# Contiguous host layouts for x, v and the first weights; the inverse's products in row-major order in DRAM; a spilled filter read in pieces of eight k1

## The chip, the cores and the metric

The kernel runs on one core of one Trainium2 chip. The metric is the time of one execution in microseconds of device time; several executions are taken and their median is given. A separate execution is recorded by the hardware profiler, and its span, from the first to the last instruction, is what all rows of the trace below refer to.

## What is computed

A long convolution, gated, and two token-wise MLPs behind it (T = 12480 tokens, D = 128 channels, d_ff = 2048):

```python
h_mlp = np.maximum(pos_emb @ w1, 0.0) @ w2
h_filt = h_mlp * np.exp(-0.01 * pos)[:, None]
u = x * v
y = irfft(rfft(u, 2 * S) * rfft(h_filt, 2 * S))[:S]
x = (x * y)
x = relu(x @ w_in) ** 2 @ w_out                 # moe
h = x @ w_in2
out = (h * sigmoid(1.702 * h)) @ w_out2          # moe2
```

The weights of the MLPs arrive as 64-bit floats; x, v and the filter's inputs as 32-bit floats.

## The kernel before

The convolution is done as a Fourier transform of length N1 x N2 = 99 x 127 in two steps, with real matrices on TensorE; the symmetric and antisymmetric halves (64 values j each) are kept apart. The stages follow each other on TensorE:

1. **Filter stage** (`filter_stage`, lines 192 to 257). Sixteen steps of four j: `stage2` multiplies the position features with w1, VectorE writes `htsb`; `stage3` multiplies with `w2s` and `w2d` (w2 twice, and w2 with its second half negated, made by VectorE at lines 224 and 225) and fills `h`. Beside it the class `Inputs` (lines 152 to 190) brings in x and v in 16 chunks of eight channels: `load` issues four DMAs a chunk (rows 0 to 95 and 96 to 98 of x and of v), `multiply` forms x*v and the even part of u on GpSimd, `odd` the odd part on VectorE. There are four buffers for x and v, and a new chunk is only asked for when the chunk four before it has had its `odd`.
2. **First transform of h** (lines 541 to 552, `s1_step`, 32 steps of four channels). Each four steps fill one `Ah`, which is written to DRAM (`ahd`, line 551). `Ah` has two buffers, so step 8 has to wait for the write of steps 0 to 3. The write is issued by SP, in order with the loads of x and v: the first stands behind the load of chunk 12, the second behind that of chunk 14.
3. **First transform of u** (lines 557 to 562, 32 steps), into `A` in SBUF. Meanwhile SP fetches the first matrices `m` and the first pieces `Hs` of the spilled filter.
4. **Second transform, product and inverse** (`stage_s2`, lines 286 to 351): 50 pairs p of frequencies k1. `spectra` multiplies `Hs` and `A` with `m` on TensorE and copies one result on ScalarE; `product` forms the complex product (VectorE, and one part on GpSimd) one pair later; `back` multiplies by the inverse matrix two pairs later, and ScalarE copies the result to `bs`, which goes to DRAM (`bd`) every two pairs (line 334). `load_m` asks for the matrices of pair p+4, `load_h` (line 279) at each odd p for the Hs of four k1 (two pairs) with number p//2+2, into one of three buffers. VectorE also converts the first MLP's weights from 64 bits here, step by step (`Weights.tick`, one step a pair); their raw chunks are fetched by `load_raw` (line 83).
5. **The MLPs** (`mlp`, lines 385 to 524). For each of 26 tiles of 480 tokens, `load_b` (line 372) reads the products `bd` back as `uv`, in 32 pieces, GpSimd forms `b`, `front_y` finishes the inverse on TensorE, and then eight units of matrix products a layer run, three passes each.

All orders are written out by hand; an engine and a DMA queue take their instructions in program order. SP issues the loads (but for w2 and two small ones) and the writes of `Ah`; ScalarE's queue issues the writes of `bd` and of the output. Lines are those of the kernel before.

Of the kernel before, what the change touches and what calls it, by code (L numbers as in the profile page):

```python
# [9 lines left out]
FP32 = mybir.dt.float32  # L10
F32R = mybir.dt.float32r
I32 = mybir.dt.int32
U32 = mybir.dt.uint32
ACTF = mybir.ActivationFunctionType
ALU = mybir.AluOpType
# [12 lines left out]
D = 128  # L28
F = 64
DFF = 2048  # L30
NP = -(-N1 // 2)
DC = 16
NDC = D // DC
XC = 8
NXC = D // XC
HK = 4
NHK = -(-N1 // HK)
JG = 2
MW = 480
NTILE = T // MW  # L40
# [20 lines left out]
def conv_mlp_kernel(ctx: ExitStack, tc: tile.TileContext, xc, xt, vc, pt, w1, w2,  # L61
# [10 lines left out]
    wj = const.tile([128, NJ], FP32, name="wj")  # L72
    sign = const.tile([128, 2], FP32, name="sign")

    bd = dram.tile([N1, 2, NJ, 2, D], FP32, name="bd")
    ahd = dram.tile([128, NDC, N1, 2, DC], FP32, name="ahd")
    raws = [moe_w_in, moe_w_out.rearrange("(k p) e -> p k e", p=128),
            moe2_w_in, moe2_w_out.rearrange("(k p) e -> p k e", p=128)]
    WC = 512
    NWC = DFF // WC  # L80
    wts = []

    def load_raw(n, pool):
        i, c = divmod(n, NWC)
        raw = pool.tile([128, WC, 2], I32, tag="raw", name="raw", bufs=2)
        if i % 2 == 0:
            nc.sync.dma_start(out=raw.rearrange("p a b -> p (a b)"),
                              in_=raws[i].bitcast(I32)[:, c * 2 * WC:(c + 1) * 2 * WC])
        else:
            k = WC // 128  # L90
            nc.sync.dma_start(out=raw.rearrange("p (k e) b -> p k (e b)", k=k),
                              in_=raws[i].bitcast(I32)[:, c * k:(c + 1) * k, :])
        return raw
# [58 lines left out]
    class Inputs:  # L152
# [6 lines left out]
        def load(self):  # L159
            c = self.loaded  # L160
            if c == NXC or c - self.odd_done == 4:
                return
            self.loaded += 1
            sl = slice(c * XC, (c + 1) * XC)
            xs, vs = (self.pool.tile([N1, XC, 2, NJ], FP32, tag=n, name=n, bufs=4) for n in ("x", "v"))
            for r in (slice(0, ROWS), slice(ROWS, N1)):
                nc.sync.dma_start(out=xs[r], in_=xc[r, sl])
                nc.sync.dma_start(out=vs[r], in_=vc[r, sl])
            self.tiles[c] = xs, vs

        def multiply(self):
# [20 lines left out]
    def filter_stage(fp, bank, h, inputs):  # L192

        HC = 4
        NC_ = NJ // HC
        bw1 = fp.tile([128, 128], FP32, name="bw1", bufs=1)
        w2s = fp.tile([128, D], FP32, name="w2s", bufs=1)
        w2d = fp.tile([128, D], FP32, name="w2d", bufs=1)
        warm = fp.tile([128, 1], FP32, name="warm", bufs=1)
        nc.vector.memset(bw1, 0.0)  # L200
        nc.vector.memset(warm, 0.0)
        p_t, ht_t = {}, {}

        def load_pos(c):
            p = fp.tile([128, HC, N1], FP32, tag="pos", name="pos", bufs=12)
            nc.sync.dma_start(out=p, in_=pt[:, c * HC:(c + 1) * HC, :])
            p_t[c] = p

        nc.scalar.activation(out=warm, in_=warm, func=ACTF.Sigmoid)
        for i in range(2):  # L210
            nc.sync.dma_start(out=bw1[i * F:(i + 1) * F, i * F:(i + 1) * F], in_=w1)
        for c in range(4):
            load_pos(c)
        for i in range(2):
            nc.scalar.dma_start(out=w2s[i * F:(i + 1) * F], in_=w2)
        nc.scalar.dma_start(out=wj, in_=c_w2)
        nc.scalar.dma_start(out=wn1, in_=c_w1)
        for c in range(4, 8):
            load_pos(c)
        inputs.load()  # L220
        nc.sync.dma_start(out=cs1, in_=c_s1)
        nc.vector.memset(sign[:, 0:1], 1.0)
        nc.vector.memset(sign[:, 1:2], -1.0)
        nc.vector.tensor_copy(out=w2d[0:F], in_=w2s[0:F])
        nc.vector.tensor_scalar(out=w2d[F:128], in0=w2s[F:128], scalar1=-1.0, scalar2=None, op0=ALU.mult)

        def stage2(c):
            ps = bank("hp")[:, 0:HC * N1].rearrange("p (j n) -> p j n", n=N1)
            nc.tensor.matmul(out=ps, lhsT=bw1, rhs=p_t.pop(c))
            sb = fp.tile([128, HC, N1], FP32, tag="ht", name="htsb")  # L230
            wb = wj[:, c * HC:(c + 1) * HC].unsqueeze(2).to_broadcast([128, HC, N1])
            nc.vector.scalar_tensor_tensor(out=sb, in0=ps, scalar=0.0, in1=wb, op0=ALU.max, op1=ALU.mult)
            ht_t[c] = sb

        def stage3(c):
            sb = ht_t.pop(c)
            ps = bank("op")[:N1].rearrange("p (s d j) -> p s d j", s=2, j=HC)
            for j in range(HC):
                for s, w in enumerate((w2s, w2d)):
                    nc.tensor.matmul(out=ps[:, s, :, j], lhsT=sb[:, j, :], rhs=w)  # L240
            nc.vector.tensor_scalar(out=h[:, :, c * HC:(c + 1) * HC], in0=ps[:, 0], scalar1=wn1[:, 0:1],
                                    scalar2=None, op0=ALU.mult)
            nc.scalar.activation(out=h[:, :, NJ + c * HC:NJ + (c + 1) * HC], in_=ps[:, 1],
                                 func=ACTF.Copy, scale=wn1[:, 0:1])

        for c in range(NC_ + 1):
            if c + 8 < NC_:
                load_pos(c + 8)
            if c < NC_:
                stage2(c)  # L250
                inputs.load()
            if c >= 1:
                stage3(c - 1)
            if c >= 1:
                inputs.multiply()
            if c in (6, 8, 9, 11, 12, 14, 16):
                inputs.odd()
# [19 lines left out]
        nc.sync.dma_start(out=m_t[p][:, 0:n], in_=c_s2[:, 2 * p:2 * p + n])  # L277

    def load_h(mp, g):
        if g >= NHK:  # L280
            return
        n = min(HK, N1 - g * HK)
        h_t[g] = mp.tile([128, NDC, HK, 2, DC], FP32, tag="Hs", name="Hs", bufs=3)
        nc.sync.dma_start(out=h_t[g][:, :, 0:n], in_=ahd[:, :, g * HK:g * HK + n])

    def stage_s2(sp, mp, A, hooks, work):

# [8 lines left out]
        with kp as kp, obp as obp:  # L296
            def spectra(p):
                n, m = pair(p), m_t[p]
                xk, hk = (kp.tile([128, 2, 2, D], FP32, tag=t, name=t) for t in ("xk", "hk"))
                for j in range(n):  # L300
                    k = 2 * p + j
                    nc.tensor.matmul(out=hk[:, j].rearrange("p c (q d) -> p q c d", d=DC),  # L302
                                     lhsT=m[:, j, 0, :], rhs=h_t[k // HK][:, :, k % HK])
                    nc.tensor.matmul(out=xk[:, j], lhsT=m[:, j, 0, :], rhs=A[:, k])  # L304
                hc = sp.tile([128, 2, 2, D], FP32, tag="hc", name="hc", bufs=2)
                nc.scalar.copy(out=hc[:, 0:n], in_=hk[:, 0:n])
                k_t[p] = xk, hc
# [16 lines left out]
            def back(p):  # L324
                n, m, P = pair(p), m_t.pop(p), P_t.pop(p)
                ob = obp.tile([128, 2, 2, D], FP32, tag="ob", name="ob")
                for j in range(n):
                    nc.tensor.matmul(out=ob[:, j], lhsT=m[:, j, 1, :], rhs=P[:, j])  # L328
                g, o = divmod(2 * p, HK)
                if o == 0:  # L330
                    bs_t[g] = sp.tile([128, HK, 2, D], FP32, tag="bs", name="bs", bufs=2)
                nc.scalar.copy(out=bs_t[g][:, o:o + n], in_=ob[:, 0:n])
                if o + n == HK or p == NP - 1:
                    nc.scalar.dma_start(
                        out=bd[HK * g:HK * g + o + n].rearrange("k h j c d -> (h j) k c d"),
                        in_=bs_t.pop(g)[:, 0:o + n])

            for p in range(NP + 2):
                if p < NP:
                    spectra(p)  # L340
                if 0 <= p - 2:
                    back(p - 2)
                load_m(mp, p + 4)
                if p % 2 == 1:
                    load_h(mp, p // 2 + 2)
                if 0 <= p - 1 < NP:
                    product(p - 1)
                work.tick(p)
                for f in hooks.get(p, ()):
                    f()  # L350
# [21 lines left out]
    def load_b(bp, t):  # L372


        last = max(p[0] for p in tile_parts(t)) // JG
        for k in range(loaded[0], last + 1):
            uv = bp.tile([N1, 2, JG, 2, D], FP32, tag="uv", name="uv", bufs=2)
            nc.sync.dma_start(out=uv, in_=bd[:, :, k * JG:(k + 1) * JG])
            b = bp.tile([N1, JG, 2, 2, D], FP32, tag="b", name="b", bufs=3)
            for s, c, op in ((0, 0, ALU.subtract), (0, 1, ALU.add), (1, 0, ALU.add), (1, 1, ALU.subtract)):  # L380
                nc.gpsimd.tensor_tensor(out=b[:, :, s, c], in0=uv[:, 0, :, c], in1=uv[:, 1, :, 1 - c], op=op)  # L381
            b_t[k] = b
        loaded[0] = last + 1
# [268 lines left out]
```

## Time and profile before

| | us |
|---|---|
| runs: median (lowest to highest) of 3 | 1493.61 (1490.3 to 1494.48) |
| profiled execution: its own time | 1490.39 |
| profiled execution: span | 1488.2 |
| TensorE busy | 1436.5 |
| VectorE busy | 1151.8 |
| ScalarE busy | 953.4 |
| GpSimd busy | 272.4 |

The busy time of an engine is the time in which it had an instruction running; idle time costs something only where the engine that sets the pace of a stage is the idle one. The execution's own time is 2.2 us longer than the span. TensorE is busy for 97% of the span, and its idle time lies in the first 325 us.

### The profile page before, as it was taken

Reading aid. Unit: us, or ns where it says so; the run is one execution under the profiler, and the core shown is the slowest. Engines: PE = TensorE matmul, PEld = TensorE weight load, DVE = VectorE, ACT = ScalarE, POOL = GpSimd, SP = SyncE. Lnnn points to the kernel's source line nnn. Section 1 sums busy time; section 2 is a strip of 40 time slices with the busy share of each in tenths; the row PEclk is TensorE's granted clock in tenths of the full one; section 3 lists DMA queues with packets and bytes.
Section 4 is the critical chain, followed back from the end, with each engine's and each line's share of the span. In section 5 each row is a group of like instructions: output and inputs, shape, how many; then the busy total and the mean of one; then the engine's idle time right before and its main releaser. Section 6 shows DMA issues by size and latency. Waiting matters only on the chain.

```text
span 1488.2 us, 17857 instructions
## 1 busy us (share of the span) xinstructions
PE 1436.5 (97%) x6994; PEld 1243.6 (84%) x6994; DVE 1151.8 (77%) x1306; ACT 953.4 (64%) x1108; POOL 272.4 (18%) x230
## 2 busy tenths in 40 slices
PE   8899988869999999999999999999999999999998
PEld 7799777758878888888888888888888888888887
DVE  5677898949988777777777777777777777777887
ACT  2355443437756677666677667677666677667776
POOL 4930322232461111111101111201112001000000
PEclk9999999979999999999999999999999999999999
DMA  9872899731210000000000000000100000000000
GB/s 227 260 314 65 255 289 292 244 106 58 78 50 29 25 7 25 25 29 25 25 7 25 25 29 25 25 8 24 36 18 25 25 8 24 7 1 7 14 14 14
DMA packets 73934, 103.71 MB, mean 70 GB/s; under 512 B 5524, under 2 KB 56026, under 8 KB 72826
## 3 DMA queue, kind: packets, MB, share of 16 engines
q1 hardware_dynamic: 56620, 83.11, 18.4%
q10 hardware_dynamic: 17230, 19.47, 3.6%
q8 instruction: 55, 0.90, 0.2%
q14 instruction: 29, 0.24, 0.1%
HBM read 70.22 MB, written 32.34 MB: 69 GB/s over the span
## 4 chain that ended last, share of the span: by engine, by line
PE 83%; DMA 9%; DVE 4%; POOL 2%; issue 1%; ACT 1%; SPq 0%; POOLq 0%; ACTq 0%; DVEq 0%
PE acc L428 12%; PE hin L429 12%; PE acc L430 12%; PE hin L430 12%; PE hin L428 12%; PE acc L429 11%; DMA Hs<-ahd 5%; PE s L264 4%; PE yps L416 4%; DMA x<-in_xc_dram 2%; PE hk L302 2%; PE xk L304 2%; PE ob L328 1%; DVE gl L465 1%; POOL b L381 1%
## 5 line engine op out<-in xcount | busy, mean ns | idle before, releaser
L465 DVE TENSOR_TENSOR gl<-g,gh 128x960 fp32r<-128x960 f32 x416 | 490.9, 1180 | 35.9 <-ACT gh L461 35.4
L445 ACT ACTIVATE g<-hin 128x960 f32<-128x960 f32 x208 | 202.5, 973 | 239.1 <-PE hin L430 238.3
L428 PE MATMUL acc<-gh,w 128*128 128x480 f32 x832 | 319.6, 384 | 0.6 <-DVE lo L404 0.6
L428 PE MATMUL hin<-hi,w 128*128 128x480 f32 x832 | 318.0, 382 | 1.4 <-ACT hi L403 1.4
L429 PE MATMUL hin<-lo,w 128*128 128x480 f32 x832 | 317.4, 381 | 0.4 <-DVE lo L404 0.4
L430 PE MATMUL acc<-gh,w 128*128 128x480 f32 x832 | 317.6, 382 | 0.0
L430 PE MATMUL hin<-hi,w 128*128 128x480 f32 x832 | 317.0, 381 | 0.0
L429 PE MATMUL acc<-gl,w 128*128 128x480 f32 x832 | 316.1, 380 | 1.0 <-DVE gl L465 1.0
L381 POOL TENSOR_TENSOR b<-uv 99x256 f32<-99x256 f32 x128 | 164.3, 1314 | 774.9 <-DMA uv<-bd 483.2
L456 DVE TENSOR_TENSOR g<-hin,g 128x960 f32<-128x960 f32 x208 | 239.8, 1153 | 57.7 <-ACT g L448 57.6
L454 DVE CAST gh<-g 128x960 fp32r<-128x960 f32 x208 | 142.6, 686 | 154.4 <-ACT g L446 154.3
L448 ACT ACTIVATE g<-hin 128x960 f32<-128x960 f32 x208 | 201.0, 966 | 84.0 <-PE hin L430 75.7
L446 ACT ACTIVATE g<-g 128x960 f32<-128x960 f32 x208 | 209.4, 1007 | 6.6
L461 ACT CAST gh<-g 128x960 fp32r<-128x960 f32 x208 | 204.5, 983 | 0.3 <-DVE g L456 0.3
L428 PEld LDWEIGHTS hin<-hi,w 128*128 128x128 f32 x832 | 156.6, 188 | 29.5 <-ACT g L445 3.3
L429 PEld LDWEIGHTS acc<-gl,w 128*128 128x128 f32 x832 | 156.5, 188 | 29.0 <-DVE gl L465 3.1
L429 PEld LDWEIGHTS hin<-lo,w 128*128 128x128 f32 x832 | 157.0, 189 | 25.9 <-DVE lo L404 0.9
L430 PEld LDWEIGHTS acc<-gh,w 128*128 128x128 f32 x832 | 156.4, 188 | 26.3
L428 PEld LDWEIGHTS acc<-gh,w 128*128 128x128 f32 x832 | 156.3, 188 | 26.2 <-DVE lo L404 1.0
L430 PEld LDWEIGHTS hin<-hi,w 128*128 128x128 f32 x832 | 156.6, 188 | 25.7
L416 PEld LDWEIGHTS yps<-ci,b 99*128 99x128 f32 x608 | 75.3, 198 | 15.3 <-POOL b L381 13.7
L416 PE MATMUL yps<-ci,b 99*128 99x98 f32 (+19 forms) x608 | 75.4, 279 | 12.0 <-POOL b L381 12.0
(58 smaller groups left out, 1185.8 us busy)
## 6 DMA issues: line engine op xcount, KB each, us to landing
ahd<-Ah SPq DMA_DIRECT2D x8, 1584.0 KB
uv<-bd SPq DMA_DIRECT2D x32, 396.0 KB
m<-in_c_s_dram SPq DMA_DIRECT2D x49, 256.0 KB
Hs<-ahd SPq DMA_DIRECT2D x24, 512.0 KB
bd<-bs ACTq DMA_DIRECT2D x24, 512.0 KB
xs<-in_xt_dram SPq DMA_DIRECT2D x26, 240.0 KB
out_dram<-o ACTq DMA_DIRECT2D x26, 240.0 KB
x<-in_xc_dram SPq DMA_DIRECT2D x16, 384.0 KB
```

The lines of the kernel that those rows point to most:

```text
L381: nc.gpsimd.tensor_tensor(out=b[:, :, s, c], in0=uv[:, 0, :, c], in1=uv[:, 1, :, 1 - c], op=op)
L416: nc.tensor.matmul(out=ps[:, o:o + w], lhsT=b[:, c, :], rhs=ci2[:, c, r:r + w], start=(c == 0), stop=(c == 1))
L428: nc.tensor.matmul(out=out, lhsT=a, rhs=hl[0], start=first, stop=False)
L429: nc.tensor.matmul(out=out, lhsT=a, rhs=hl[1], start=False, stop=False)
L430: nc.tensor.matmul(out=out, lhsT=b, rhs=hl[0], start=False, stop=last)
L445: nc.scalar.activation(out=g, in_=ps, func=ACTF.Relu)
L446: nc.scalar.activation(out=g, in_=g, func=ACTF.Square)
L448: nc.scalar.activation(out=g, in_=ps, func=ACTF.Sigmoid, scale=1.702)
L454: nc.vector.tensor_copy(out=gh, in_=g)
L456: nc.vector.tensor_tensor(out=g, in0=ps, in1=g, op=ALU.mult)
L461: nc.scalar.copy(out=gh, in_=g)
L465: nc.vector.tensor_tensor(out=gl, in0=g, in1=gh.bitcast(FP32), op=ALU.subtract)
```

## The change

Six edits. (1) The host lays x and v out as [chunk, row, channel, half, j], so that one chunk of eight channels is one contiguous stretch; each row's piece keeps its 4 KB, but the rows, which lay 64 KB apart, now lie 4 KB apart. (2) The two `w_in` are laid out in four chunks of 512 columns, each contiguous; a row's piece keeps its 4 KB and the pitch goes from 16 KB to 4 KB. (3) `bd` is laid out as [half, j, k1, part, channel] in place of [k1, half, j, part, channel]: a write of four k1 has one piece of 4 KB a partition in place of four of 1 KB, and a read has pieces of 1 KB in place of 2 KB, next to each other in place of 128 KB apart. (4) A load of `uv` becomes two DMAs, one for each half. (5) `Hs` holds eight k1 (four pairs) in place of four, in two buffers in place of three, and is asked for at p = 3, 7, 11, ...; the piece goes from 512 B to 1 KB. (6) VectorE makes `w2d` after its first step of `stage2` instead of before it.

```diff
-    bd = dram.tile([N1, 2, NJ, 2, D], FP32, name="bd")
+    bd = dram.tile([2, NJ, N1, 2, D], FP32, name="bd")
...
             nc.sync.dma_start(out=raw.rearrange("p a b -> p (a b)"),
-                              in_=raws[i].bitcast(I32)[:, c * 2 * WC:(c + 1) * 2 * WC])
+                              in_=raws[i].bitcast(I32)[c])
...
-            sl = slice(c * XC, (c + 1) * XC)
             xs, vs = (self.pool.tile([N1, XC, 2, NJ], FP32, tag=n, name=n, bufs=4) for n in ("x", "v"))
             for r in (slice(0, ROWS), slice(ROWS, N1)):
-                nc.sync.dma_start(out=xs[r], in_=xc[r, sl])
-                nc.sync.dma_start(out=vs[r], in_=vc[r, sl])
+                nc.sync.dma_start(out=xs[r], in_=xc[c, r])
+                nc.sync.dma_start(out=vs[r], in_=vc[c, r])
...
-        nc.vector.tensor_copy(out=w2d[0:F], in_=w2s[0:F])
-        nc.vector.tensor_scalar(out=w2d[F:128], in0=w2s[F:128], scalar1=-1.0, scalar2=None, op0=ALU.mult)
...
                 stage2(c)
                 inputs.load()
+            if c == 0:
+                nc.vector.tensor_copy(out=w2d[0:F], in_=w2s[0:F])
+                nc.vector.tensor_scalar(out=w2d[F:128], in0=w2s[F:128], scalar1=-1.0, scalar2=None,
+                                        op0=ALU.mult)
...
-        if g >= NHK:
+        if g >= NHL:
             return
-        n = min(HK, N1 - g * HK)
-        h_t[g] = mp.tile([128, NDC, HK, 2, DC], FP32, tag="Hs", name="Hs", bufs=3)
-        nc.sync.dma_start(out=h_t[g][:, :, 0:n], in_=ahd[:, :, g * HK:g * HK + n])
+        n = min(HL, N1 - g * HL)
+        h_t[g] = mp.tile([128, NDC, HL, 2, DC], FP32, tag="Hs", name="Hs", bufs=2)
+        nc.sync.dma_start(out=h_t[g][:, :, 0:n], in_=ahd[:, :, g * HL:g * HL + n])
...
-                                     lhsT=m[:, j, 0, :], rhs=h_t[k // HK][:, :, k % HK])
+                                     lhsT=m[:, j, 0, :], rhs=h_t[k // HL][:, :, k % HL])
...
-                        out=bd[HK * g:HK * g + o + n].rearrange("k h j c d -> (h j) k c d"),
+                        out=bd[:, :, HK * g:HK * g + o + n].rearrange("h j k c d -> (h j) k c d"),
...
-                if p % 2 == 1:
-                    load_h(mp, p // 2 + 2)
+                if p % 4 == 3:
+                    load_h(mp, p // 4 + 2)
...
-            nc.sync.dma_start(out=uv, in_=bd[:, :, k * JG:(k + 1) * JG])
+            for h in range(2):
+                nc.sync.dma_start(out=uv[:, h], in_=bd[h, k * JG:(k + 1) * JG].rearrange("j k c d -> k j c d"))
...
-    laid['xc'] = _folded(x).transpose(0, 3, 1, 2)
-    laid['vc'] = _folded(v).transpose(0, 3, 1, 2)
+    for name, a in (('xc', x), ('vc', v)):
+        laid[name] = _folded(a).transpose(3, 0, 1, 2).reshape(NXC, XC, N1, 2, NJ).transpose(0, 2, 1, 3, 4)
+    for name in ('moe_w_in', 'moe2_w_in'):
+        laid[name] = inputs[name].reshape(D, NWC, WC).transpose(1, 0, 2)
```

Here HL = 8, NHL = 13, HK = 4, DC = 16, JG = 2.

How the order of the issues moves is shown at three places. The first is SP's queue in the second transform; `m` is the matrices of a pair, `Hs` a piece of the spilled filter, `raw` a chunk of raw weights. Before:

```order
L87 DMA raw<-in_moe_w_in_dram 128x1024
L277 DMA m<-in_c_s_dram 128x512
L284 DMA Hs<-ahd 128x8x128
L277 DMA m<-in_c_s_dram 128x512 x2
L284 DMA Hs<-ahd 128x8x128
L277 DMA m<-in_c_s_dram 128x512 x2
L284 DMA Hs<-ahd 128x8x128
L91 DMA raw<-in_moe_w_out_dram 128x4x256
L277 DMA m<-in_c_s_dram 128x512 x2
L284 DMA Hs<-ahd 128x8x128
```

The same place with the change:

```order
L88 DMA raw<-in_moe_w_in_dram 128x1024
L279 DMA m<-in_c_s_dram 128x512 x3
L286 DMA Hs<-ahd 128x8x256
L279 DMA m<-in_c_s_dram 128x512 x2
L92 DMA raw<-in_moe_w_out_dram 128x4x256
L279 DMA m<-in_c_s_dram 128x512 x2
L286 DMA Hs<-ahd 128x8x256
L279 DMA m<-in_c_s_dram 128x512 x4
L286 DMA Hs<-ahd 128x8x256
```

An Hs stood behind every second m and now stands behind every fourth, with twice the bytes. The second place is SP's queue where the MLPs begin; `xs` is a tile of x for the gating. Before:

```order
L378 DMA uv<-bd 99x2x512 x2
L87 DMA raw<-in_moe_w_in_dram 128x1024
L370 DMA xs<-in_xt_dram 128x480
L378 DMA uv<-bd 99x2x512
L91 DMA raw<-in_moe_w_out_dram 128x4x256
```

The same place with the change:

```order
L381 DMA uv<-bd 99x2x256 x4
L88 DMA raw<-in_moe_w_in_dram 128x1024
L372 DMA xs<-in_xt_dram 128x480
L381 DMA uv<-bd 99x2x256 x2
L92 DMA raw<-in_moe_w_out_dram 128x4x256
```

Four issues stand ahead of the raw chunk in place of two, with the same bytes in all. The third place is the start of VectorE's work. Before:

```order
L223 MEMSET sign 128x1
L224 COPY w2d<-w2s 64x128
L225 TENSOR_SCALAR w2d<-w2s 64x128
L232 SCALAR_TENSOR_TENSOR htsb<-hp,wj 128x396 x2
L241 TENSOR_SCALAR h<-op,wn_62 99x128x4
```

The same place with the change:

```order
L223 MEMSET sign 128x1
L230 SCALAR_TENSOR_TENSOR htsb<-hp,wj 128x396
L251 COPY w2d<-w2s 64x128
L252 TENSOR_SCALAR w2d<-w2s 64x128
L230 SCALAR_TENSOR_TENSOR htsb<-hp,wj 128x396
L239 TENSOR_SCALAR h<-op,wn_62 99x128x4
```

The two instructions on w2d have moved behind the first htsb.

## Rows read from the trace of the kernel before

**Rows 1.** The page's part 4, the chain that ended last, by line

```profile
PE acc L428 12%; PE hin L429 12%; PE acc L430 12%; PE hin L430 12%; PE hin L428 12%; PE acc L429 11%; DMA Hs<-ahd 5%; PE s L264 4%; PE yps L416 4%; DMA x<-in_xc_dram 2%; PE hk L302 2%; PE xk L304 2%; PE ob L328 1%; DVE gl L465 1%; POOL b L381 1%
```

**Rows 2.** Windows: stretch, length, busy PE, PEld, DVE, ACT, POOL, clock, DMA share, GB/s

```profile
0.00:40.00 40.00, 34.84 (x238) 29.27 (x238) 20.51 (x36) 9.73 (x14) 18.73 (x19) 1.00 0.92 228
40.00:80.00 40.00, 31.35 (x180) 29.18 (x178) 21.96 (x28) 13.83 (x19) 39.30 (x29) 0.91 0.90 279
...
148.00:300.00 152.00, 132.69 (x592) 110.72 (x592) 137.37 (x214) 62.28 (x108) 43.32 (x50) 1.00 0.85 268
300.00:325.00 25.00, 15.14 (x62) 12.64 (x63) 6.00 (x7) 7.23 (x9) 11.95 (x16) 0.60 0.47 143
...
454.00:1488.00 1034.00, 1030.27 (x4940) 888.83 (x4938) 797.38 (x809) 731.46 (x812) 103.67 (x88) 1.00 0.06 20
```

**Rows 3.** Timelines of ACT and PE, 48 to 84 us: start, length, instructions, idle before

```profile
67.99 2.96 ACT L266 COPY Ah<-s 64x792 f32<-64x792 f32 x4 [7.00 <-DMA ahd<-Ah]
78.37 2.96 ACT L266 COPY Ah<-s 64x792 f32<-64x792 f32 x4 [7.42 <-DMA ahd<-Ah]
...
48.70 9.65 PE L264 MATMUL s<-cs,h 99*128 99x198 f32 x56 [1.56 <-ACT h L243]
...
69.88 7.86 PE L264 MATMUL s<-cs,h 99*128 99x198 f32 x32 [4.08 <-DVE Ah L268]
80.26 4.04 PE L264 MATMUL s<-cs,h 99*128 99x198 f32 x14 [2.52 <-DVE Ah L268]
```

**Rows 4.** SP in order of time, 58 to 70 us

```profile
58.62 0.32 SPq L167 DMA_DIRECT2D x<-in_xc_dram  x1
...
60.16 0.36 SPq L551 DMA_DIRECT2D ahd<-Ah  x1
...
69.68 0.35 SPq L551 DMA_DIRECT2D ahd<-Ah  x1
```

**Rows 5.** GpSimd in order of time, 37 to 59 us

```profile
37.01 2.51 POOL L178 TENSOR_TENSOR x<-x,v 99x512 f32<-99x512 f32 x2 [2.95 <-DMA v<-in_vc_dram]
...
56.82 1.77 POOL L180 TENSOR_TENSOR u<-x 99x512 f32<-99x512 f32 x1
```

**Rows 6.** DMA queues, 10 to 50 us: packets, MB, share of 16

```profile
q1 hardware_dynamic: 3556, 9.59, 96.9%
```

**Rows 7.** DMA queues of 341 to 345 us, one weight chunk alone

```profile
q1 hardware_dynamic: 144, 0.52, 44.5%
```

**Rows 8.** DMA queues of 88 to 106 us, mostly writes of Ah

```profile
q1 hardware_dynamic: 464, 5.07, 67.5%
```

**Rows 9.** Waits of 148 to 300 us: in total, times, longest

```profile
PE hk L302 <- DMA Hs<-ahd: 16.2, 16, 2.2
DVE t L315 <- ACT hc L306: 12.5, 16, 2.4
```

**Rows 10.** VectorE in order of time, 150 to 158 us

```profile
150.24 1.29 DVE L315 TENSOR_TENSOR t<-xk,hc 128x512 f32<-128x512 f32 x2 [1.84 <-ACT hc L306]
...
156.38 1.29 DVE L315 TENSOR_TENSOR t<-xk,hc 128x512 f32<-128x512 f32 x2 [0.84 <-ACT hc L306]
```

**Rows 11.** The chain that ended last in order of time: two of eleven loads of Hs

```profile
157.33 5.97 DMA Hs<-ahd
...
248.16 7.45 DMA Hs<-ahd
```

**Rows 12.** DMA queues of 160 to 290 us (q10 is ScalarE's queue)

```profile
q1 hardware_dynamic: 31579, 26.19, 67.3%
q10 hardware_dynamic: 11281, 11.19, 24.4%
```

**Rows 13.** The chain in order of time at the change of stage

```profile
299.20 2.54 DMA bd<-bs
301.87 5.29 DMA uv<-bd
```

**Rows 14.** Instructions on tile uv: least, median, longest ns

```profile
L378 SPq DMA_DIRECT2D uv<-bd x32: 780/801/936, 301.9 to 1227.2; - x32
```

More of the change, by code (lines that the diff above doesn't have):

```diff
@@ L30 @@
 DFF = 2048
+WC = 512
+NWC = DFF // WC
 NP = -(-N1 // 2)
@@ L36 @@
 HK = 4
-NHK = -(-N1 // HK)
+HL = 8
+NHL = -(-N1 // HL)
 JG = 2
@@ L78, in conv_mlp_kernel @@
             moe2_w_in, moe2_w_out.rearrange("(k p) e -> p k e", p=128)]
-    WC = 512
-    NWC = DFF // WC
     wts = []
```

## The prediction

> **What bounds the kernel now.** I read the chain that ended last first, to see which transfers are on it: loads of Hs hold 5% of the span and loads of x 2% [rows 1], though part of that time TensorE works beside them. Next come the stretches of the stages: from 454 us on TensorE is busy for 1030.27 of 1034 us, so nothing that a DMA does can shorten the MLPs [rows 2]. Time can only be won ahead of 325 us, in three places.
>
> Place A, 60 to 82 us, is the first transform of h. ScalarE may not fill the third and fourth `Ah` until the writes of the first and second have landed: 7.00 and 7.42 us [rows 3]. TensorE rests for 4.08 and 2.52 us of this, and is slow behind it: 56 matmuls in 9.65 us are 0.172 us each when it is not held up, so the 32 in 7.86 us lose 2.35 us and the 14 in 4.04 us lose 1.63 us [rows 3]; the granted clock of the stretch 40 to 80 us is 0.91 [rows 2]. Together TensorE loses 4.08 + 2.52 + 2.35 + 1.63 = 10.6 us. The write is late because SP issues it behind the load of chunk 12 (58.62, then 60.16 us), and the second behind chunk 14 (69.68 us) [rows 4]. That load waits for a buffer which GpSimd frees: chunk 8 ends at 56.82 + 1.77 = 58.59 us [rows 5]. GpSimd works without a pause from 37.01 us, and started there because v of chunk 4 had not come (2.95 us of waiting) [rows 5]. So the rate of the x and v loads before 37 us sets the time of the writes.
>
> Place B, 148 to 300 us, is the second transform. TensorE waits for Hs 16 times, 16.2 us, but VectorE, 137.37 us busy of 152, is the fuller engine, and it waits for the copy of that product 12.5 us in 16 waits [rows 2, 9]. The first two of these, 1.84 and 0.84 us, are the start of the pipeline [rows 10]; 9.8 us are left that come from Hs. A load takes 5.97 to 7.45 us from issue to landing [rows 11]. It is asked for at p = 2g-3 and needed at p = 2g, so two whole pairs lie between, 2 x 2.65 = 5.3 us (132.69 us over 50 pairs) [rows 2]: too few.
>
> Place C, 299 to 308 us, is the change to the MLPs: the last write of bd takes 2.54 us and the first uv 5.29 us, one after the other [rows 13].
>
> **The change part by part.** The sum is made on the profiled execution, 1490.39 us. The three runs shown have a median of 1493.61; the four times together average 1492.2, and I start from that: the profile gives the differences, 1492.2 the level.
>
> Hs in eights: SP issues 13 loads in place of 25. The load at p = 4g-5 is needed at p = 4g, four whole pairs later, which is 4 x 2.75 = 11.0 us at VectorE's pace (137.37 / 50). A load has 0.52 MB more, 2.0 us at 268 GB/s [rows 2], so it lands after 8.0 to 9.5 us (5.97 and 7.45 plus 2.0). It is in time by 1.5 us or more, and the 9.8 us vanish; VectorE is then the bound and no more than that can come. The DMA engines must keep up: in 160 to 290 us the two queues took 67.3% + 24.4% = 91.7% of 16 engines for 37.4 MB [rows 12]. In 121 us the same packet time would be 98.5%. Half the packets of Hs and a quarter of those of bd make it less; at the rate of long pieces (below, 26 KB/us an engine) it would be 74%. I take 9 us, nearly all, as the lead is certain and the room small; the ends are 0 and 9.8, and a loss is a rival below.
>
> x and v contiguous: from 10 to 50 us the engines were full, 0.969 x 16 x 40 = 620 engine-us for 9.59 MB, which is 15.5 KB/us an engine [rows 6]. A weight chunk, alone, with the same 4 KB pieces but 16 KB apart, took 0.445 x 16 x 4 = 28.5 engine-us for 0.52 MB, 18.2 KB/us [rows 7]. Writes with pieces of 12.7 KB ran at 5.07 MB in 194 engine-us, 26.1 KB/us [rows 8]. Those three are the bounds: no gain, 18.2, and 26.1. I take 18.2, the row nearest in piece and direction. The first five chunks are 5 x 0.81 = 4.06 MB: 262 engine-us become 223, and 39 / 16 = 2.4 us; at 26.1 it would be 6.6 us. GpSimd's unbroken row begins 2.4 us earlier, and with it SP's issue of the writes. Chunks 12 to 15 share the engines with the first two writes; their 3.24 MB cost 209 engine-us and would cost 178, 1.9 us less ahead of the second write. I take 2.4 + 1.9, rounded down to 4 us. The ends are 0 and 10.6, all that is lost in place A. Nothing is late next: GpSimd and then TensorE go on without a gap.
>
> One rule speaks against this term. The Trainium skill, "DMA: Bandwidth & Descriptors", section on latency and other measured facts, says that a row pitch of large powers of two slows HBM, with full rate still at 512 KiB and a loss from 2 MiB on. By it 64 KB costs nothing, and the 4 us would be 0. The rows show a slower stream at 64 KB than at 16 KB [rows 6, 7], though not that the pitch is the reason.
>
> bd and uv: a write of bd takes a quarter of the packets; it lies beside other work except for the last one. The last uv is on the path. Its issue costs 0.80 us [rows 14], and a second issue adds up to 0.8 us ahead of GpSimd; two for the second piece, 1.6 us. Against that stand pieces next to each other: if it landed as fast as bd's write, 2.54 in place of 5.29 us [rows 13], 2.75 us would be saved. I take 0, between -1.9 and +1.6. Later uv loads are hidden by the MLPs' 1030 us of matmuls [rows 2]; 32 more issues on SP, 26 us over 1034, have nobody behind them in a hurry.
>
> w_in in contiguous chunks: VectorE is not seen waiting for a raw chunk, so 0; what hides it is the conversion of the chunk before. w2d behind the first htsb: VectorE is busy 20.51 of 40 us there [rows 2], and the first consumer comes behind w2s; 0.
>
> The sum is 9 + 4 + 0 = 13 us: 1477.4 on the profiled execution, 1479 at the level of 1492.2.
>
> **The rivals.**
> 1. The layout of x and v brings nothing, since the distance of the rows is not what makes the stream slow. Then 1492.2 - 9 = 1483. The rule of the Trainium skill named above would have it so. For it: the mixed stream of 10 to 50 us has other loads in it. Against: the row of the weight chunk.
> 2. Place B brings nothing, as the DMA engines are full and the same bytes take the same time; Hs stays late in another rhythm. Then 1492.2 - 4 = 1488. For it: 98.5% above. Against: fewer packets.
> 3. Neither does what it says: 1492.
> 4. Slower. An Hs of 1.05 MB, with a raw chunk of 0.52 MB ahead of it, holds up what stands behind it on SP's queue, the m of the next pairs. If SP's queue got only half of the 268 GB/s while ScalarE's queue writes bd, the two take 11.7 us and 2.5 us to land, 14.2 in all, 3.2 us over the 11.0 of lead. Seven raw chunks make 22 us, five loads without one 1 us each: 27 in place of 9.8, so 1492.2 + 17 - 4 = 1505. It decides from about 185 GB/s on SP's queue downward (1.57 MB in 8.5 us). Against: over 130 us that queue had 26.19 MB, 201 GB/s [rows 12], and the bytes of a raw chunk come once in six pairs.
>
> **How the numbers follow.** My forecast has a chance of 0.62, rival 1 0.18, rival 2 0.08, rival 3 0.07, rival 4 0.05. A measurement of this kernel can tell about 0.3%, 4.5 us, from no change: the border lies near 1488. Forecast and rival 1 are faster, half of rival 2 too: 0.84. The other half and rival 3 are within: 0.11. Slower is rival 4: 0.05. With both terms at their upper ends the time is 1492.2 - 20.4 = 1472, with uv's end 1470 and the level 2 us lower 1468. The upper end takes in rivals 1 and 2: 1488. Left out are rivals 3 and 4 and some of the tails, under 2 in 10.
>
> **What would show it.** Right: in 148 to 300 us TensorE waits for Hs 3 us or less in sum, and VectorE for `hc` about 3 us; the stage ends about 9 us sooner after its start. GpSimd's unbroken row starts near 34.5 us, the first write of Ah is issued near 57.5 us, ScalarE's two waits shrink to about 4 to 6 us each. From 10 to 50 us the engines move 18 KB/us or more. Wrong: waits for m in the second transform (rival 4), waits for Hs of the old size (rival 2), 15.5 KB/us again (rival 1), or a first uv that lands later than 7 us after its issue.

## The result, and the profile after

| | before | after |
|---|---|---|
| runs: median (lowest to highest), us | 1491.95 (1490.21 to 1494.48), 4 runs | 1477.49 (1476.27 to 1478.08), 4 runs |
| profiled execution: its own time, us | 1490.39 | 1478.08 |
| profiled execution: span, us | 1488.2 | 1475.9 |

The ratio is 0.9902, with a 95% interval of 0.9886 to 0.9918: 14.5 us by the medians, 12.3 us by the two profiled spans. The forecast was 1479.0. In the chain that ended last, loads of Hs held 5% of the span and of x 2% [rows 1]; neither is among its lines now. For Hs that is the gain shown below. For x it is not: the chain of the kernel after still holds loads of x and v for 23% of its first 110 us, a little under 1% of the span each. The page's part 4 of the kernel after, by line:

```profile
PE acc L431 12%; PE acc L433 12%; PE hin L432 12%; PE hin L433 12%; PE hin L431 12%; PE acc L432 12%; PE yps L419 4%; PE s L266 4%; PE ob L330 2%; DVE t L317 1%; PE xk L306 1%; PE hk L304 1%; DMA ahd<-Ah 1%; POOL b L384 1%; DVE gl L468 1%
```

Shares do not say where the 12.3 us are. I cut both executions at the same four events: the first product `hk` of the second transform, the issue of the last write of `bd`, and the first `yps` of the MLPs.

| stretch | before, us | after, us | less by |
|---|---|---|---|
| span's start to first `hk` (place A in it) | 147.11 | 146.74 | 0.4 |
| first `hk` to last issue of `bd` (place B) | 299.20 - 147.11 = 152.1 | 287.81 - 146.74 = 141.1 | 11.0 |
| last issue of `bd` to first `yps` (place C) | 308.10 - 299.20 = 8.9 | 294.96 - 287.81 = 7.15 | 1.75 |
| first `yps` to the end | 1180.1 | 1180.9 | -0.8 |

**Place B.** The waits of the second transform, in the stretch 130 to 300 us of the kernel after (engine, line and what it waited for; us in total, times, longest):

```profile
POOL P L321 <- DVE t L317: 75.8, 41, 2.5
...
PE ob L330 <- POOL P L321: 5.2, 11, 1.4
...
DVE t L317 <- ACT hc L308: 2.7, 2, 1.8
...
PE hk L304 <- DMA m<-in_c_s_dram: 0.9, 1, 0.9
```

There is no wait for Hs any more; before it was 16.2 us on TensorE [rows 9]. VectorE waited 16 times for `hc`, 12.5 us; two waits of 2.7 us are left, the two that belong to the start of the pipeline [rows 10]. TensorE now waits for the products `P`, which GpSimd makes behind VectorE's `t`. One window over exactly this stretch (columns as in [rows 2]):

```profile
146.70:287.80 141.10, 133.87 (x594) 111.81 (x594) 136.22 (x214) 61.96 (x108) 43.32 (x50) 0.99 0.82 281
```

VectorE is busy for 136.22 of 141.10 us: it is the bound, as foreseen. The stage's 11.0 us are the 9.8 us of waits and 1.2 us by which VectorE's own work became shorter (137.42 us over the same stretch before). The DMA queues, 160 to 280 us (packets, MB, share of 16 engines):

```profile
q1 hardware_dynamic: 20152, 25.65, 66.2%
q10 hardware_dynamic: 3179, 11.56, 23.6%
```

25.65 MB in 0.662 x 16 x 120 engine-us is 20.2 KB/us an engine; before it was 18.7 (26.19 MB in 0.673 x 16 x 130, [rows 12]). ScalarE's queue went from 22.0 to 25.5.

**Place A.** ScalarE and TensorE in order of time, 66 to 89 us of the kernel after, to be held against [rows 3] (start, length, instructions, and in brackets the idle time before):

```profile
67.06 2.96 ACT L268 COPY Ah<-s 64x792 f32<-64x792 f32 x4 [6.37 <-DMA ahd<-Ah]
77.40 2.96 ACT L268 COPY Ah<-s 64x792 f32<-64x792 f32 x4 [7.38 <-DMA ahd<-Ah]
...
68.95 8.96 PE L266 MATMUL s<-cs,h 99*128 99x198 f32 x32 [3.45 <-DVE Ah L270]
79.29 2.95 PE L266 MATMUL s<-cs,h 99*128 99x198 f32 x16 [1.38 <-DVE Ah L270]
```

ScalarE's two waits were 7.00 and 7.42 us and are 6.37 and 7.38. The start of GpSimd's unbroken row and SP's issue of the first two writes moved as little (37.01 us in [rows 5]; 60.16 and 69.68 us in [rows 4]). GpSimd and then SP of the kernel after:

```profile
36.65 2.55 POOL L178 TENSOR_TENSOR x<-x,v 99x512 f32<-99x512 f32 x2 [3.01 <-DMA v<-in_vc_dram]
...
59.85 0.36 SPq L554 DMA_DIRECT2D ahd<-Ah  x1
...
68.56 0.35 SPq L554 DMA_DIRECT2D ahd<-Ah  x1
```

The reason is in the DMA queues of 10 to 50 us:

```profile
q1 hardware_dynamic: 3573, 9.63, 96.2%
```

9.63 MB in 0.962 x 16 x 40 = 616 engine-us is 15.6 KB/us an engine, where it was 15.5 [rows 6]. The x and v stream did not become faster by being contiguous.

**Place C.** The chain in order of time of the kernel after:

```profile
287.81 2.54 DMA bd<-bs
290.84 3.19 DMA uv<-bd
```

The chain had 5.29 us for the first uv [rows 13] and has 3.19. The two are not counted alike: the 5.29 begin with the issue, the 3.19 behind the first of two issues. From the landing of the last `bd` to that of the first uv it is 307.16 - 301.74 = 5.42 us before and 294.03 - 290.35 = 3.68 us after, issues included. The four issues now take 1.64 us on SP for two pieces, as two issues at 0.80 did [rows 14].

So the total came near the forecast by errors of opposite sign, which is luck and no merit of the sum: of the sum of 13 us, place A fell short by 3.6, places B and C gave 2.0 and 1.75 beyond their terms, and 0.8 went behind the first `yps`: 12.3 us between the two profiled spans.

### The profile page after: what moved, and what is told of

It is laid out like the page before. It is cut to its first block, busy times and chain, and to the rows that moved or that the text cites. A ratio compares the mean times of both kernels' runs of the same rounds, so it can differ in the third digit from the quotient of the medians.

```text
span 1475.9 us, 17869 instructions
## 1 busy us (share of the span) xinstructions
PE 1437.7 (97%) x6994; PEld 1246.0 (84%) x6994; DVE 1153.5 (78%) x1306; ACT 952.8 (65%) x1108; POOL 263.1 (18%) x230
## 4 chain that ended last, share of the span: by engine, by line
PE 84%; DVE 6%; DMA 5%; POOL 2%; ACT 1%; issue 1%; SPq 0%; POOLq 0%; ACTq 0%
PE acc L431 12%; PE acc L433 12%; PE hin L432 12%; PE hin L433 12%; PE hin L431 12%; PE acc L432 12%; PE yps L419 4%; PE s L266 4%; PE ob L330 2%; DVE t L317 1%; PE xk L306 1%; PE hk L304 1%; DMA ahd<-Ah 1%; POOL b L384 1%; DVE gl L468 1%
## 5 line engine op out<-in xcount | busy, mean ns | idle before, releaser
L384 POOL TENSOR_TENSOR b<-uv 99x256 f32<-99x256 f32 x128 | 155.1, 1242 | 781.4 <-DMA uv<-bd 493.6
L432 PEld LDWEIGHTS hin<-lo,w 128*128 128x128 f32 x832 | 157.3, 189 | 25.5 <-DVE lo L407 0.5
L433 PEld LDWEIGHTS acc<-gh,w 128*128 128x128 f32 x832 | 156.5, 188 | 26.1
L419 PEld LDWEIGHTS yps<-ci,b 99*128 99x128 f32 x608 | 75.1, 198 | 14.0 <-POOL b L384 12.5
```

The source lines that it names most:

```text
L419: nc.tensor.matmul(out=ps[:, o:o + w], lhsT=b[:, c, :], rhs=ci2[:, c, r:r + w], start=(c == 0), stop=(c == 1))
L432: nc.tensor.matmul(out=out, lhsT=a, rhs=hl[1], start=False, stop=False)
L433: nc.tensor.matmul(out=out, lhsT=b, rhs=hl[0], start=False, stop=last)
```

## The experiments

Every time is a median with a 95% interval of the ratio to the kernel before, run on the same chip. The kernel after stands at 0.9902. Differences to the kernel after in us are between medians from several chips; the kernel before had medians of 1490.24 to 1491.95 us there.

**1. Hs in eights, alone.** The kernel before, with this part of the change and no other:

```diff
-        h_t[g] = mp.tile([128, NDC, HK, 2, DC], FP32, tag="Hs", name="Hs", bufs=3)
+        h_t[g] = mp.tile([128, NDC, HL, 2, DC], FP32, tag="Hs", name="Hs", bufs=2)
...
-                if p % 2 == 1:
-                    load_h(mp, p // 2 + 2)
+                if p % 4 == 3:
+                    load_h(mp, p // 4 + 2)
```

> The kernel before with one edit of the change alone: Hs in pieces of eight k1, two buffers, asked for at p = 3, 7, 11. Theory (the gain is Hs arriving in time in the second transform, the layouts of x and v give nothing): 11 us less than before, VectorE's waits for hc near 2.7 us in place of 12.5, and the first matmul of the MLPs 8 to 9 us behind the last write of bd as before. Rival (the other edits carry part of the second transform, by shorter packet time of bd's writes): 5 us or less.

Measured 1478.44 us, ratio 0.992 (0.9897 to 0.9943). The second transform took 286.86 - 146.21 = 140.65 us, and VectorE's waits in it are those of the kernel after (waits, 130 to 315 us):

```profile
DVE t L316 <- ACT hc L307: 2.7, 2, 1.8
```

Nearly the whole gain is this one part.

**2. Longer pieces, or an earlier issue?** The eights do two things at once: pieces of 1 KB in place of 512 B, and a lead of four pairs in place of two. Here the kernel before keeps its fours and its 25 loads, and asks one group sooner, with a fourth buffer:

```diff
-        h_t[g] = mp.tile([128, NDC, HK, 2, DC], FP32, tag="Hs", name="Hs", bufs=3)
+        h_t[g] = mp.tile([128, NDC, HK, 2, DC], FP32, tag="Hs", name="Hs", bufs=4)
...
-                    load_h(mp, p // 2 + 2)
+                    load_h(mp, p // 2 + 3)
...
-                if d // 4 in (10, 14):
+                if d // 4 in (10, 14, 18):
```

> The kernel before, Hs in pieces of four k1 as before (512 B pieces), but with four buffers and asked for one group earlier, so that four whole pairs lie between issue and use in place of two. If the lead is what counts: 10 to 11 us less than before, the same as with eight k1. If the length of the pieces (512 B to 1 KB) counts: under 4 us less, and waits of TensorE for Hs stay above 8 us.

Measured 1478.43 us, ratio 0.9919 (0.9896 to 0.9941). The waits, 130 to 315 us:

```profile
DVE t L315 <- ACT hc L306: 2.7, 2, 1.8
```

The lead alone does it; the length of the piece is not needed.

**3. Eights with the old lead.** The other half of that pair: the kernel after, where Hs is asked for two pairs before it is needed.

```diff
-                if p % 4 == 3:
-                    load_h(mp, p // 4 + 2)
+                if p % 4 == 1 and p > 4:
+                    load_h(mp, p // 4 + 1)
```

> The changed kernel, but Hs of eight k1 asked for at p = 5, 9, 13, two whole pairs ahead of its use in place of four. If the lead is what counts: each of the eleven loads is 2 to 4 us late, TensorE waits for Hs 20 us or more in sum, 12 to 30 us slower than the changed kernel, no faster than before. If the length of the pieces counts: within 4 us of the changed kernel.

Measured 1504.0 us, ratio 1.0095 (1.0064 to 1.0125): 26.5 us above the kernel after and slower than before. The waits, 130 to 315 us:

```profile
PE hk L304 <- DMA Hs<-ahd: 26.3, 11, 2.9
DVE t L317 <- ACT hc L308: 16.4, 12, 2.5
DVE t L317 <- PE xk L306: 9.7, 3, 4.3
```

and one of its loads in the chain in order of time:

```profile
162.49 7.51 DMA Hs<-ahd
```

7.5 us from issue to landing do not fit into two pairs of 2.7 us; the fours, which landed in 5.58 to 7.45 us, did not fit either. VectorE waits 16.4 + 9.7 = 26.1 us in place of 2.7, and the stage is 312.78 - 147.09 = 165.7 us long, 24.6 us over the 141.1.

**4. x and v with the old rows.** The kernel after, with x and v laid out as before; this is the part that was forecast at 4 us.

```diff
-                nc.sync.dma_start(out=xs[r], in_=xc[c, r])
+                nc.sync.dma_start(out=xs[r], in_=xc[r, c * XC:(c + 1) * XC])
...
-        laid[name] = _folded(a).transpose(3, 0, 1, 2).reshape(NXC, XC, N1, 2, NJ).transpose(0, 2, 1, 3, 4)
+        laid[name] = _folded(a).transpose(0, 3, 1, 2)
```

> The changed kernel with x and v laid out as before (rows of a chunk 64 KB apart in place of 4 KB). Theory (the distance of the rows does not set the rate): the time of the changed kernel within 1.5 us, 15 to 16 KB/us an engine from 10 to 50 us. Rival (the layout helps and something else takes it back): 3 us or more slower than the changed kernel, with GpSimd's unbroken row of multiplications starting later than 37 us.

Measured 1478.05 us, ratio 0.9915 (0.9888 to 0.9943), no difference from the kernel after. The queues of 10 to 50 us:

```profile
q1 hardware_dynamic: 3559, 9.58, 96.8%
```

15.5 KB/us with rows 64 KB apart, 15.6 with rows 4 KB apart. The Trainium skill, "DMA: Bandwidth & Descriptors", section on latency and other measured facts, gives 207 GB/s at a pitch of 512 KiB beside 214 where a pitch of 4 MiB was padded by 4 KiB, and less from 2 MiB on. That nothing is lost at 64 KB in this pair agrees with it.

**5. bd and uv as before.** The kernel after with the old layout of `bd` and one DMA a piece:

```diff
-    bd = dram.tile([2, NJ, N1, 2, D], FP32, name="bd")
+    bd = dram.tile([N1, 2, NJ, 2, D], FP32, name="bd")
...
-            for h in range(2):
-                nc.sync.dma_start(out=uv[:, h], in_=bd[h, k * JG:(k + 1) * JG].rearrange("j k c d -> k j c d"))
+            nc.sync.dma_start(out=uv, in_=bd[:, :, k * JG:(k + 1) * JG])
```

> The changed kernel with the products bd laid out as before and uv read by one DMA of 2 KB pieces that lie 128 KB apart. Theory (the new layout gives 1 to 2 us at the change to the MLPs and nothing in the second transform, which VectorE bounds): 1 to 3 us slower than the changed kernel, the last bd write to the first yps about 8.9 us in place of 7.15, the second transform as long as in the changed kernel. Rival (shorter packet time of the bd writes helps the second transform): it gets 2 us or more longer there.

Measured 1478.69 us, ratio 0.9926 (0.991 to 0.9942). By the medians 1.2 us, which cannot be told from nothing; the trace can tell it. The chain at the change of stage:

```profile
287.02 2.78 DMA bd<-bs
289.91 4.92 DMA uv<-bd
```

From the last issue of `bd` to the first `yps` it takes 295.76 - 287.02 = 8.74 us, 1.6 more than the kernel after. The other traces bear it out: the same step takes 8.4 and 8.3 us in runs 1 and 2, which have the old layout too, and 6.9 to 7.3 us in all the runs with the new one. The second transform is 287.02 - 146.43 = 140.6 us, no longer than with the new layout: the shorter packet time of `bd`'s writes buys nothing there.

**6. x and v over 128 partitions.** If the distance of the rows does not set the rate, the number of rows may: 99 rows were read as 96 + 3. The kernel after, with x and v padded on the host to 128 rows that are read in one DMA; only the first 99 are computed with.

```diff
-            for r in (slice(0, ROWS), slice(ROWS, N1)):
+            for r in (slice(0, 128),):
...
+        laid[name] = np.pad(laid[name], ((0, 0), (0, 128 - N1), (0, 0), (0, 0), (0, 0)))
```

> The changed kernel with x and v padded on the host to 128 rows, so that a chunk is two DMAs over 128 partitions in place of four over 96 and 3; 29% more bytes, 29 rows of them unused. If the 96 rows set the rate: 19 to 21 KB/us an engine from 10 to 50 us, as a weight chunk alone has (20.4), GpSimd's row starts no later than 36.7 us in spite of the bytes, and the time is within 2 us of the changed kernel. If the kind of stream sets it (4 KB reads behind each other at 15.6 KB/us): 15 to 16 KB/us, GpSimd's row starts 2 us or more later, 2 to 6 us slower.

Measured 1476.88 us, ratio 0.9911 (0.9893 to 0.9929). The queues of 10 to 50 us, and GpSimd's row:

```profile
q1 hardware_dynamic: 4117, 12.07, 83.2%
```

```profile
15.27 2.50 POOL L178 TENSOR_TENSOR x<-x,v 99x512 f32<-99x512 f32 x2 [14.83 <-DMA v<-in_vc_dram]
17.84 1.26 POOL L180 TENSOR_TENSOR u<-x 99x512 f32<-99x512 f32 x1
19.06 2.50 POOL L178 TENSOR_TENSOR x<-x,v 99x512 f32<-99x512 f32 x2
```

12.07 MB in 0.832 x 16 x 40 engine-us is 22.7 KB/us an engine: x and v have 29% more bytes, and they arrive sooner. GpSimd works almost without a pause from 15 us, not from 37. And yet the time is the same. ScalarE in place A of this kernel:

```profile
66.68 2.96 ACT L268 COPY Ah<-s 64x792 f32<-64x792 f32 x4 [5.91 <-DMA ahd<-Ah]
75.43 2.96 ACT L268 COPY Ah<-s 64x792 f32<-64x792 f32 x4 [5.79 <-DMA ahd<-Ah]
83.16 2.96 ACT L268 COPY Ah<-s 64x792 f32<-64x792 f32 x4 [4.77 <-DMA ahd<-Ah]
```

The first write is issued at 57.23 us, 2.6 us sooner, but ScalarE resumes only 0.4 us sooner, and a third wait of 4.77 us comes behind the two. From issue to landing that write takes 9.34 us, where the kernel after has 7.11. The first `hk` comes at 148.32 us, no sooner than with the change alone. In both kernels the DMA engines are full from 60 to 80 us (the last two columns are their share and GB/s); first the kernel after, then this one:

```profile
60.00:80.00 20.00, 15.14 (x68) 14.22 (x67) 10.54 (x11) 6.25 (x9) 19.61 (x16) 0.83 1.02 367
60.00:80.00 20.00, 15.27 (x80) 14.66 (x79) 11.52 (x14) 6.69 (x9) 17.86 (x14) 0.91 1.00 410
```

This trace has to be read with care: its execution took 1482.25 us, the other three of the run 1475.58 to 1477.16. And part of what it lost went with the clock: its last 96 matmuls on `h` took 19.81 us, where its first 96 took 16.35, and the granted clock from 85 to 105 us was 0.83. That the padding gains no more than the spread is shown by the medians, 1476.88 and 1477.49 us, and by runs 11 and 12 below.

**7. The writes of Ah on ScalarE's queue,** one step late, so that no load of x stands ahead of them:

```diff
+                if d % DC == 0 and d:
+                    nc.scalar.dma_start(out=ahd[:, d // DC - 1], in_=Ap)
...
-                if (d + 4) % DC == 0:
-                    nc.sync.dma_start(out=ahd[:, d // DC], in_=Ah)
+                Ap = Ah
...
```

> The changed kernel with the writes of Ah issued on ScalarE's queue, one step after the tile is full, instead of on SP behind the loads of x and v. Theory (the first two writes are late because SP's queue stands at a load that waits for a buffer): the first write is issued near 57 us in place of 59.85, the second near 63 to 65 in place of 68.56, ScalarE's two waits of 6.4 and 7.4 us shrink by 3 us each, the second transform begins 4 to 7 us earlier and the time is 4 to 7 us less. Rival (the DMA engines are full between 58 and 80 us, so an earlier issue lands no earlier): within 1.5 us.

A miss: 1481.18 us, ratio 0.9943 (0.9925 to 0.9961), 3.7 us more than the kernel after. ScalarE in order of time:

```profile
63.66 0.81 ACT L268 COPY Ah<-s 64x792 f32<-64x792 f32 x1 [2.67 <-DMA ahd<-Ah]
63.73 0.33 ACTq L550 DMA_DIRECT2D ahd<-Ah  x1
71.75 0.81 ACT L268 COPY Ah<-s 64x792 f32<-64x792 f32 x1 [5.13 <-DMA ahd<-Ah]
75.75 0.33 ACTq L550 DMA_DIRECT2D ahd<-Ah  x1
```

The write at 63.73 stands behind the copy that waited until 63.66 for the write before it. So one write is in flight at a time; they go out at 63.73, 75.75, 83.67 and 91.98 us. The queue that I moved it to had a wait of its own.

**8. VectorE relieved.** The kernel after, with the product's subtraction on GpSimd: if VectorE is the new bound of the second transform, the stage must become shorter.

```diff
-                nc.vector.tensor_tensor(out=P[:, 0:n, 0], in0=t[0][:, 0:n, 0], in1=t[1][:, 0:n, 1],
+                nc.gpsimd.tensor_tensor(out=P[:, 0:n, 0], in0=t[0][:, 0:n, 0], in1=t[1][:, 0:n, 1],
...
```

> The changed kernel with the second part of the complex product (a subtraction, 50 times 0.42 us) moved from VectorE to GpSimd. Theory (VectorE sets the pace of the second transform): VectorE has 21 us less, TensorE with 134 us becomes the bound, 3 to 7 us less. Rival (GpSimd's 0.87 us in place of 0.42 lies on the way to the inverse matmul, or slows VectorE beside it): no gain, or 2 to 6 us slower.

Measured 1471.63 us, ratio 0.9875 (0.9854 to 0.9896), 5.9 us less than the kernel after. A window over its second transform:

```profile
148.20:284.10 135.90, 130.50 (x594) 112.29 (x594) 101.08 (x164) 61.70 (x108) 81.76 (x100) 0.99 0.85 292
```

135.9 us in place of 141.1, VectorE busy for 101.08 in place of 136.22, and TensorE, 130.50 us, is the fullest engine. VectorE was the bound.

**9. A third buffer of Ah.** The kernel after with one word changed:

```diff
-        with tc.tile_pool(name="stg", bufs=2, side="right", reuse_waits="tile") as stg:
+        with tc.tile_pool(name="stg", bufs=3, side="right", reuse_waits="tile") as stg:
```

> The changed kernel with three buffers of Ah in place of two, everything else and every issue as it is. Theory (the first transform of h is held up by the landing of the writes, with two buffers, whoever issues them): step 8 no longer waits for the first write; the waits of 6.4 and 7.4 us become one or two of under 4 us, the second transform begins 5 to 9 us earlier than 146.7 us and the time is 5 to 9 us less. Rival (the DMA engines are the bound there, full from 58 to 80 us): the waits only move to later tiles, 2 us or less won.

Measured 1470.06 us, ratio 0.9861 (0.9846 to 0.9875), 7.4 us less than the kernel after. ScalarE and TensorE, 48 to 97 us:

```profile
76.26 2.96 ACT L268 COPY Ah<-s 64x792 f32<-64x792 f32 x4 [3.89 <-DMA ahd<-Ah]
83.03 3.03 ACT L268 COPY Ah<-s 64x792 f32<-64x792 f32 x4 [3.81 <-DMA ahd<-Ah]
...
48.48 16.35 PE L266 MATMUL s<-cs,h 99*128 99x198 f32 x96 [1.56 <-ACT h L241]
65.61 11.58 PE L266 MATMUL s<-cs,h 99*128 99x198 f32 x64 [0.77 <-DVE Ah L270]
78.15 1.61 PE L266 MATMUL s<-cs,h 99*128 99x198 f32 x8 [0.96 <-DVE Ah L270]
```

ScalarE waits for writes of `Ah` twice, 7.7 us, where the kernel after waits five times, 19.9 us. The first two writes are issued hardly sooner than in the kernel after (59.03 and 68.33 us against 59.85 and 68.56). The first `hk` starts at 139.63 us in place of 146.74. The same 20 us as shown under run 6:

```profile
60.00:80.00 20.00, 17.96 (x101) 16.44 (x100) 14.46 (x17) 9.78 (x13) 19.69 (x15) 1.00 1.00 366
```

The granted clock is 1.00 here, 2.4 GHz throughout. In the kernel after it is 0.83, and 0.53 from 72 to 76 us, close to the level of 1.2 GHz; its TensorE rested 3.45 us ahead of the slow 32 matmuls shown under place A. So the number of buffers held place A: a third one shortens it by 7.1 us with x and v arriving as before, and with DMA engines that are just as full.

**10. Is it the three-row DMAs?** In run 6 two things were taken away: the 96-row DMA and the DMA of the three rows behind it. Here x and v are padded to 112 rows and read as 96 + 16:

```diff
-            for r in (slice(0, ROWS), slice(ROWS, N1)):
+            for r in (slice(0, ROWS), slice(ROWS, 112)):
...
+        laid[name] = np.pad(laid[name], ((0, 0), (0, 112 - N1), (0, 0), (0, 0), (0, 0)))
```

> The changed kernel with x and v padded to 112 rows, read in four DMAs a chunk of 96 and 16 rows in place of 96 and 3. If the DMAs of three rows, which cannot use all engines, made the stream slow (22.7 KB/us an engine with 128 rows in one DMA, 15.6 with 96 and 3): 20 KB/us or more from 10 to 50 us. If the 96 rows do: 15 to 17 KB/us.

Measured 1481.29 us, ratio 0.9935 (0.9915 to 0.9956). The queues of 10 to 50 us:

```profile
q1 hardware_dynamic: 3841, 9.92, 103.2%
```

15.0 KB/us: no better with 16 rows than with 3, so it is not the three rows. What is left, as far as was tried, is the 96-row read itself, or the cutting of a chunk into four DMAs in place of two; no run parts these, and why either should be slow stays open. The other loads of that stretch are slow with it: by the packet records a piece of `pos`, 1584 B and over 128 partitions in every kernel, takes 99 ns in the kernel after and 67 in run 6 (medians). The time is 3.8 us above the kernel after (two executions): in the trace the first two writes of `Ah` are issued at 61.78 and 72.55 us, and the first `hk` comes at 152.0 us. With two buffers, then, later loads went with a longer place A, although earlier ones (run 6) gained nothing.

**11 and 12. All that helped, together.** Run 11 is the kernel after with the edits of runs 6, 8 and 9; run 12 leaves out the padding (8 and 9).

> The changed kernel with three edits together: x and v padded to 128 rows, the second part of the product on GpSimd, three buffers of Ah. If they add up (0.6 + 5.9 us measured, and 5 to 9 us for the buffers, which with faster loads of x and v have less in front of them): 1462 to 1468 us. Rival (one bound hides the other, or TensorE rests and slows again after a shorter stall): 1468 to 1474.

> The change with the product's subtraction on GpSimd and a third buffer of Ah, and x and v as the change has them (no padding). Theory: the two gains lie in different stages, each behind its own bound, so they add: 5.9 + 7.4 = 13.3 us less than the change, 1464 us; the start of the second transform near 139.6 us, its length near 135.9 us; the padding of the run with all three cost about 3 us. Rival: they do not add, because with the earlier start something behind the second transform takes part of it back (the first MLP tiles' start, the raw weights); then 1466 to 1468 us, as in the run with all three edits, and the padding made no difference.

Run 11 measured 1466.86 us, ratio 0.9834 (0.9813 to 0.9854); run 12 1468.16 us, ratio 0.9831 (0.9804 to 0.9857). The two cannot be told apart, so the padding of x and v is worth nothing here either. Both beat the kernel after by about 10 us. By the ratios the gains add up: run 8 stands 0.0027 and run 9 0.0041 below the kernel after, 0.0068 in sum, and run 11 stands 0.0068 and run 12 0.0071 below it. By the profiled spans, one execution each, run 8 is 4.3 and run 9 7.6 us shorter than the kernel after, 11.9 in sum, and run 12 (span 1466.4) is 9.5 shorter; but the five executions of run 12 lie between 1465.14 and 1468.58 us, so the missing 2.4 us are not shown to be more than spread. In the trace its second transform takes 277.80 - 140.20 = 137.6 us, 1.7 more than in run 8. The waits of TensorE in it, 140 to 280 us, of run 12:

```profile
PE hk L304 <- DMA m<-in_c_s_dram: 4.3, 3, 2.3
PE ob L330 <- POOL P L322: 2.0, 2, 1.6
```

In run 8 the wait for `m` was 2.2 us, in the kernel after 0.9. The 2.1 us more than in run 8 would cover the 1.7, but that is argued from one trace each; no run asks for `m` sooner.

## Why the prediction was right, and where it was not

**Place B: right, by its own steps.** The claim was that two pairs of lead are too few for the landing of Hs and four are enough (the eleven loads in the chain before took 5.58 to 7.45 us, a little wider than the two that were read), that the 9.8 us of VectorE's waits vanish, and that VectorE is the bound behind it. Runs 1, 2 and 3 show the lead to be the cause: early fours gain the same as eights, and eights with the old lead cost 26.5 us. Run 8 shows VectorE's bound. The term was 9 us, its upper end 9.8, and 11.0 were found; the end was too low because it held VectorE's own work to be fixed, and that became 1.2 us shorter (136.22 in place of 137.42). It is shorter in the traces without waits for Hs, whatever the layouts (135.75 to 136.25 us in runs 1, 2 and 5), and not in run 3, which has them (137.25): it goes with the waits.

**Place A: the step that failed is "x and v contiguous", 4 us.** It failed twice. I took 18.2 KB/us from the weight chunk as "the row nearest in piece and direction"; but that row differs from the x stream in more than the pitch: it has 128 partitions against 96, and it ran alone. Run 4 shows that the pitch does nothing (15.5 and 15.6), run 6 that reading 128 rows in one DMA does (22.7). Rival 1 had this part right. And the step behind it, from faster loads to earlier writes of `Ah` to a shorter place A, did not hold either: in run 6 the loads move half as much again per busy engine-us and the first write is issued 2.6 us sooner, and the median gains 0.6 us, within the spread. "Nothing is late next" was wrong: the landing of the writes is late next (9.34 us in run 6, 7.11 in the kernel after). Run 9 shows what the row of waits really said: ScalarE waits for a write to land because it has two buffers, and a third takes 7.4 us away.

**Place C: the mechanism was named, the term mis-sized.** I took 0 between -1.9 and +1.6; the trace shows 1.75 us less, and run 5 gives 1.6 of it to the layout of `bd` with its two reads a piece. The faster landing outweighs the added issues (5.42 to 3.68 us with both in it), since four issues of half the size take 1.64 us together, not 0.8 each.

**Terms of nothing.** From the first `yps` on both kernels take 1180 to 1181 us, so later uv loads, the 32 added issues on SP and the later `w_in` chunks together cost and bring nothing beyond 0.8 us. Moving `w2d` was not run alone, but shows nothing either: the first `hk` comes 0.4 us sooner for all edits ahead of it.

**The rivals.** Rival 1 held for its part, but not for its total of 1483, since B and C gave more than their terms. Rivals 2 and 3 fall with run 1. Rival 4, an Hs that holds up `m`, is not in the kernel after (one wait for `m` of 0.9 us); that run 3 comes out near its price of about 1505 us is chance, since there it is Hs that is late.

## What to carry to other kernels

A prefetch is sized by holding its issue-to-landing time, under the load of its own stage, against the time between issue and need; if it is too short, ask sooner; once both were asked for early, the length of the pieces made no difference here. Where an engine waits for a write to land before it may fill the buffer again, count the buffers first and only then look for what delays the write. A rate taken from another transfer has to be checked for what else differs: here it was not the pitch but the partitions, or the number of DMAs that go with them. And a DMA moved to another queue inherits whatever that queue's engine waits for.

## What was not expected of the hardware

From 10 to 50 us, when nearly all that is loaded is x, v and `pos`, the queue moved 15.0 to 15.6 KB/us an engine with x and v read over 96 partitions, and the DMA engines were 96% to 103% busy in the records, whatever the distance of the rows and whether 3 or 16 rows followed; with the same pieces of 4 KB over 128 partitions in one DMA it moved 22.7, 83% busy. A busy DMA engine is therefore not one at its best rate. The uv read of 99 partitions, from the landing of the write before it to its own, took 3.68 us as two DMAs with adjacent pieces of 1 KB, and 5.42 as one with pieces of 2 KB lying 128 KB apart.
